# Seven-product matrix multiplication in a token mixer: the third of seven products is itself computed by seven, and the second weights' even and odd rows get separate buffers

## The chip, the cores and the metric

The kernel runs on one core of one Trainium2 chip. The metric is the device time of one execution in microseconds (us). One core has TensorE (matmuls, called PE in the profile; PEld is its weight load), VectorE (DVE), ScalarE (ACT), GpSimd (POOL), SyncE (SP, which here only issues transfers) and DMA engines. All timed executions quoted here are with a granted TensorE clock of 0.999 or 1.0.

## The reference, cut to what matters

Two blocks run one after the other: linear attention, then a token mixer. Only the second half of the mixer (the code calls it mixer 2) is touched:

```python
u = einsum("bsd,sf->bdf", layernorm(h), w1) + b1      # mixer 1
u = gelu(u)
y = einsum("bdf,fs->bds", u, w2) + b2                 # mixer 2: F = 3584, S = 2048, D = 1024
h2 = h + y.transpose(0, 2, 1)
```

## The kernel before

Mixer 2 multiplies w2 by u with a seven-product scheme in the manner of Strassen: a 2x2 block product is done with seven block products in place of eight, at the price of sums of blocks. A `Product7` works on one pair of output row tiles. Its products are p1 to p7: each is 14 matmuls of 128x128 weights by 512 columns. PSUM is the memory in which TensorE accumulates; its matmuls hold one operand (the weights) and stream the other (the moving operand). Products accumulate in place in PSUM tiles A, B, C, so that copying A to B and B to C carries shared partial sums on. The sums of weight blocks (`asums(m)`, for product m) and of the moving operand are made by DVE. A read-out is the operation of DVE or ScalarE that takes the finished partial sum of an inner product out of PSUM; "read-out 7" is that of inner product 7. An evacuation takes a finished output block out and adds the bias.

A product can be computed by seven products again. `Inner` does that for the same product of two neighbouring tile pairs together (a "Quad"): 2 x 14 = 28 wide matmuls become 7 x 7 = 49 matmuls of 256 columns, which is 49 x 256 = 12,544 columns in place of 28 x 512 = 14,336. Products 1 and 5 of mixer 2 are done so in the kernel before. In mixer 2 `Inner.banks` is 2: the inner partial sums a and e are halves of one PSUM tile, b and c halves of another.

```python
class Inner:
    ...
    def i1(self):
        ae = psz.tile([P, BANK], F32, tag="z0", bufs=1, name="psI0")
        bc = psz.tile([P, BANK], F32, tag="z1", bufs=1, name="psI1")
        e = ... if self.banks == 4 else ae
        self.a, self.e, self.b, self.c = ae[:, 0:HW], e[:, HW:CW], bc[:, 0:HW], bc[:, HW:CW]
        self.mm(1, self.a, True)
        act.copy(self.b, self.a)
    def i2(self):
        self.mm(2, self.a, False)
        self.sink(0, 0, self.a)               # read-out 2
    def i5(self): self.mm(5, self.e, True); ...
    def i7(self): self.mm(7, self.c, False); ...   # read-out 7
    def i3(self): self.mm(3, self.b, False); ...
class Inner2(Inner): ...                      # read-outs add into a given tile
```

The narrow matmuls of an inner block are interleaved with wide matmuls of another product ("fill"), in this order:

```python
for f in (n.i1, "b", 0, n.i6, "c", n.i2, 1, n.i5, n.i7, "7", 2, n.i3, "third", 3, n.i4, "end"):
    ...   # an integer is a stretch of fill (9, 7, 5, 7 matmuls here); a name is a place for other engines' work
```

A round of mixer 2 (one Quad; there are three, after a first pair of tile pairs that uses plain products) was:

```python
def run2(self, pend, nxt, on_p4, on_p7, cut):
    ...
    self.interleave(self.in1, self.steps(*[st.p4 for st in pend]))   # inner block of product 1
    on_p4()
    ...
    self.asums(7)
    self.interleave(in5, self.steps(*[st.p6 for st in sts]))         # inner block of product 5
    self.asums(3)
    nxt = nxt()
    for st in sts: st.p2()
    ...
    if nxt is not None: nxt.begin2()      # weight sums of product 5, inner sums of product 1
    for st in sts: st.p7(...)
    on_p7()                               # moving operand of product 4, 2 DVE operations of 2 us
    for st in sts: st.p3()
```

## Time and profile before

| | before |
|---|---|
| time, median (range) | 566.55 us (566.08 to 566.8) |
| TensorE busy | 557.5 of 564.1 us |
| DVE busy | 431.5 us |
| one round of mixer 2 | 40.92 us |

The page of the kernel before: busy time by engine, and the shares of the chain that ended last.

```profile
PE 557.5 (99%) x3215; PEld 303.6 (54%) x3215; DVE 431.5 (76%) x822; ACT 281.5 (50%) x597; POOL 1.8 (0%) x8
...
PE 96%; DVE 2%; ACT 1%; issue 0%; DVEq 0%; ACTq 0%
```

TensorE is in 96% of the chain. This is the chain in order of time around the first round (start in us, duration in us, engine, tile, line, matmuls):

```profile
431.96 0.77 PE psI L217 x7
...
454.75 6.04 PE psA L217 x28
460.79 6.04 PE psC L217 x28
466.83 6.04 PE psB L217 x28
472.88 0.77 PE psI L217 x7
```

These pieces follow one another without a gap, so in mixer 2 the time is simply the sum of the matmuls. It also gives the cadence: 28 wide matmuls take 6.04 us, 216 ns each, and 7 narrow ones 0.77 us, 109 ns each. The Trainium skill, "TensorE: Matmul & The Clock Gate", section "Wait — 56ns, not 53.3ns?", gives N / 2.4 GHz plus about 2.5 ns for a warm matmul, from which 215.8 and 109.2 ns follow as estimates for 512 and 256 columns; the trace agrees with its 216 and 109. The "mean ns" of 379 and 273 that the groups show are lengths of overlapping, pipelined matmuls and no cadence.

What TensorE waited for at inner products in the whole kernel (total us, times, longest):

```profile
PE psI L217 <- DVE t L217: 0.6, 1, 0.6
PE psI L217 <- ACT psI L217: 0.4, 1, 0.4
```

Both are in mixer 1; mixer 2 has none. DVE has room in the first round (its operations in order of time, with the idle time before each in brackets):

```profile
452.85 2.21 DVE L217 TENSOR_TENSOR sa<-wq,sa 128x1792 f16<-128x1792 bf16 x2
458.53 0.43 DVE L217 TENSOR_TENSOR ot<-ot,hr 128x512 bf16<-128x512 bf16 x1 [3.47 <-ACT ot L474]
```

Between 455.1 and 458.5 us DVE had nothing to do. In the second round's first inner block the read-out of inner product 7 also found DVE idle, for 1.24 us:

```profile
480.26 0.43 DVE L217 TENSOR_TENSOR psA<-psI,es 128x256 f32<-128x256 f32 x1 [1.24 <-PE psI L217]
```

### The profile page before, as it was taken

To read this page: it belongs to the slowest core of one execution; us is meant where nothing else is said; L and a number is where in the kernel's file an instruction comes from. 1 tells how busy PE (TensorE), PEld (TensorE's weight loads), DVE (VectorE), ACT (ScalarE), POOL (GpSimd) and SP (SyncE) were. 2 spreads that over 40 slices of the span, in tenths; PEclk is the share of its full clock that TensorE was granted. 3 is DMA by queue.
4 is the path that set the end of the run, shared out by engine and by line. 5 is a ranking of instruction groups with operands and counts; after the bars stand their busy time and mean duration, and the time that the engine had idled before them with its cause. 6 is when DMAs were issued, how large, how long until landed. Compare 5 with 4: busy or idle time off the path is not lost.

```text
span 564.1 us, 8558 instructions
## 1 busy us (share of the span) xinstructions
PE 557.5 (99%) x3215; PEld 303.6 (54%) x3215; DVE 431.5 (76%) x822; ACT 281.5 (50%) x597; POOL 1.8 (0%) x8
## 2 busy tenths in 40 slices
PE   8999999999999999999999999999999999999997
PEld 3444444454444444456667766666445655645643
DVE  6898888544776788888989789888979749658725
ACT  5747777757766877635546465565211311311211
POOL 1000000000000000000000000000000000000000
PEclk9999999999999999999999999999999999999999
DMA  9933332125674852104040340432983922912111
GB/s 304 294 76 75 87 82 38 19 58 194 206 215 123 266 173 80 69 1 125 27 149 21 130 150 1 150 82 50 249 218 94 265 72 75 296 42 74 38 48 46
DMA packets 86089, 67.15 MB, mean 119 GB/s; under 512 B 15762, under 2 KB 80032, under 8 KB 86048
## 3 DMA queue, kind: packets, MB, share of 16 engines
q1 hardware_dynamic: 85312, 65.94, 40.8%
q10 hardware_dynamic: 672, 0.66, 0.3%
q8 instruction: 25, 0.41, 0.3%
q14 instruction: 16, 0.13, 0.1%
q0 software_dynamic: 64, 0.01, 0.0%
HBM read 54.54 MB, written 8.91 MB: 112 GB/s over the span
## 4 chain that ended last, share of the span: by engine, by line
PE 96%; DVE 2%; ACT 1%; issue 0%; DVEq 0%; ACTq 0%
PE psI L217 19%; PE acc_t L217 18%; PE psC L217 15%; PE psB L217 11%; PE psA L217 4%; PE psB L877 4%; PE psC L877 4%; PE psA L877 4%; PE acc_t L801 3%; PE psB L333 2%; PE psA L333 2%; PE acc_t L1152 2%; PE psE L877 2%; PE psC L333 2%; PE kvps L830 1%; PE psE L333 1%
## 5 line engine op out<-in xcount | busy, mean ns | idle before, releaser
L217 PEld LDWEIGHTS <-wq 128*128 128x128 bf16 (+1 forms) x629 | 61.1, 98 | 45.7
L217 PEld LDWEIGHTS <-sa 128*128 128x128 f16 x627 | 61.3, 98 | 36.7 <-issue 0.9
L217 PEld LDWEIGHTS <-is 128*128 128x128 f16 x568 | 55.4, 98 | 27.1 <-issue 1.8
L217 PE MATMUL acc_t<-wo_sb,pqT 128*128 128x512 f16 x256 | 55.6, 379 | 0.0
L217 PE MATMUL psC<-gs,wq 128*128 128x512 f16 (+2 forms) x210 | 44.9, 365 | 0.0
L217 PE MATMUL acc_t<-xnT,wq_sb 128*128 128x512 bf16 x192 | 43.4, 379 | 0.0
L217 PEld LDWEIGHTS <-pqT 128*128 128x128 bf16 x256 | 24.9, 98 | 30.5 <-issue 0.6
L179 DVE TENSOR_SCALAR e_sb<-e_sb 128x512 bf16<-128x512 bf16 x64 | 18.6, 290 | 28.7 <-ACT e_sb L175 28.2
L175 ACT ACTIVATE e_sb<-acc_t 128x512 bf16<-128x512 f32 x40 | 23.9, 597 | 24.5 <-PE acc_t L217 12.0
L217 DVE TENSOR_TENSOR ot<-ot,hr 128x512 bf16<-128x512 bf16 (+2 forms) x27 | 11.2, 414 | 28.1 <-ACT ot L474 27.7
L877 PEld LDWEIGHTS <-xs 128*128 128x128 f16 x208 | 20.0, 98 | 23.4 <-DVE xs L863 1.3
L217 PE MATMUL psC<-hT,sa 128*128 128x512 f16 x112 | 31.2, 379 | 0.0
L217 PEld LDWEIGHTS <-wq_sb 128*128 128x128 bf16 x192 | 18.5, 98 | 23.0 <-issue 1.3
L217 PE MATMUL psI<-hi,is 128*128 128x256 f16 x200 | 30.0, 272 | 0.4 <-ACT psI L217 0.4
L217 PE MATMUL psB<-hT,sa 128*128 128x512 f16 x112 | 29.7, 379 | 0.0
L217 DVE BATCH_NORM_STATS2 hst<-acc_t 128x6 f32<-128x512 f32 x32 | 21.4, 693 | 9.0 <-ACT h_bf L217 8.9
L877 PE MATMUL psA<-wkv,xnT 128*128 128x512 bf16 x104 | 26.7, 379 | 0.0
L877 PEld LDWEIGHTS <-xnT 128*128 128x128 bf16 x156 | 15.3, 98 | 18.5 <-issue 0.2
L217 PE MATMUL psC<-hT,wq 128*128 128x512 f16 x96 | 24.6, 379 | 0.0
L217 ACT CAST h_bf<-acc_t 128x512 bf16<-128x512 f32 x32 | 18.4, 581 | 12.0 <-PE acc_t L217 12.0
L217 ACT COPY psI<-psI 128x256 f32<-128x256 f32 x50 | 18.0, 359 | 11.6 <-PE psI L217 10.5
L176 ACT ACTIVATE r_sb<-acc_t 128x512 bf16<-128x512 f32 x40 | 23.7, 592 | 0.0
(214 smaller groups left out, 1033.5 us busy)
## 6 DMA issues: line engine op xcount, KB each, us to landing
wq<-in_B_w_dram SPq DMA_DIRECT2D x14, 1024.0 KB, 7.9
wq<-in_B_w_dram SPq DMA_DIRECT2D x8, 1792.0 KB, 10.3
xr<-in_A_x_dram SPq DMA_DIRECT2D x16, 256.0 KB, 5.2
rdb<-rd_dram SPq DMA_DIRECT2D x32, 128.0 KB, 4.0
h_dram<-h_bf SPq DMA_DIRECT2D x16, 256.0 KB, 2.0
hr<-h_dram SPq DMA_DIRECT2D x32, 128.0 KB, 2.6
out_dram<-ot SPq DMA_DIRECT2D x31, 128.0 KB, 1.7
x_sb<-in_A_x_dram SPq DMA_DIRECT2D x15, 256.0 KB, 3.1
```

The lines of the kernel that those rows point to most:

```text
L175: pin(nc.scalar.activation(e_sb[:], src, ACT.Exp))
L176: pin(nc.scalar.activation(r_sb[:], src, ACT.Relu))
L179: pin(nc.vector.tensor_scalar(e_sb[:], e_sb[:], 1.0, PHI_EPS, ALU.min, ALU.add))
L217: return (lambda *a, **kw: pin(op(*a, **kw))) if self.always or getattr(Held, self.key) else op
L333: pe.matmul(ps[:, cols], lhsT=lhs[:, k, :], rhs=mv(k)[:, cols], start=(start and k == 0), stop=(k == self.nk - 1), skip_group_check=True,)
L801: mm = nc.tensor.matmul(pp[:, 0:CW], lhsT=xnT[:, kt, i * P:(i + 1) * P], rhs=wkv[:, kt, c * CW:(c + 1) * CW], start=(kt == 0), stop=(kt == ...
L830: pin(nc.tensor.matmul(kv_ps[b][:, sl, :], lhsT=pks[i % NPK][:, j * P:(j + 1) * P], rhs=vaugs[i % NVA][:, j, :], start=False, stop=(i == N ...
L877: pin(nc.tensor.matmul(ps[:], lhsT=lhs[:, k, :], rhs=rhs[:, k, :], start=(start and k == 0), stop=(k == hk2 - 1), skip_group_check=True,))
L1152: nc.tensor.matmul(qp[:, 0:SW], lhsT=wq_sb[:, kt, j * P:(j + 1) * P], rhs=xnT[:, kt, u * SW:(u + 1) * SW], start=(kt == 0), stop=(kt == ND ...
```

## The change

Product 3 is computed by a third inner block (`in3`), interleaved with p2 as fill; p7 moves in front of it. This needs four new sums of the moving operand, once (`sums3`), and four inner sums of weights in each round. Its read-outs are added into the tile e by DVE. The weights of the even row blocks of w2 are free once p7 is through; so they get single buffers that are reloaded there, which makes room for the new tiles. The interleaving order gets one more place for other engines' work, "2", right after inner product 2. The core of the diff, cuts marked, comments added:

```diff
+    def load_w2(p, second):
         nc.sync.dma_start(
-            w2_tiles[p],
-            B_w2[:, p * 2 * P:(p + 1) * 2 * P].rearrange("(k p) s -> p k s", p=P),
+            (odd[p] if second else even[p % 2]),
+            B_w2[:, p * 2 * P:(p + 1) * 2 * P].rearrange("(k two p) s -> p k two s", two=2, p=P)[:, :, second, :],
         )
 ... (cut)
+        def run2(self, pend, on_p4, on_p7, cut, third_sums):
+            def starting():
+                self.asums(5)
+                self.in5 = self.inner(5)
+                self.in5.sums()
+                self.asums(6)
+                for st in sts:
+                    st.begin()
+            self.interleave(self.in1, self.steps(*[st.p4 for st in pend]), {"b": starting}, ...)
             on_p4()
 ... (cut)
             self.asums(7)
-            self.interleave(in5, self.steps(*[st.p6 for st in sts]))
+            self.interleave(self.in5, self.steps(*[st.p6 for st in sts]))
+            third_sums()                       # first round only: four DVE operations
             self.asums(3)
+            in3 = Inner2(sts, 3, self.mov3, "i", self.add_to(e), None)
+            in3.sums()
             for st in sts:
-                st.p2()
+                st.p7()
+                dve.tensor_tensor(st.e[:], st.B[:], st.e[:], ALU.add)
 ... (cut)
+            nxt, halves = on_p7()              # issues the loads of the next even weights
+            halves[0]()                        # product 4's moving operand, first half
+            self.interleave(in3, self.steps(*[st.p2 for st in sts]), {
+                "2": halves[1], "7": begin_next, "third": before_last, "end": ...,
+            }, (("7", None),))
-            for st in sts:
-                st.p3()
```

In the first pair of tile pairs the products stay as they were, but both p7 now come before the last p2, and the next pair's even weights are loaded after them.

More of the change, by code (lines that the diff above doesn't have):

```diff
@@ L152, in load_w1, with w2_view, first_w2 @@
         ))
-    def load_w2(p, pool):
-        w2_tiles[p] = w_tile(pool, WLEN if pool is wpool else NF * 2 * P)[:, 0:NF * 2 * P].rearrange("p (k f) -> p k f", f=2 * P)
+    WH = NFP * 2 * P
+    even, odd = {}, {}
+    def w2_view(t):
+        return t.rearrange("p (k f) -> p k f", f=2 * P)
+    def load_w2(p, second):
         nc.sync.dma_start(
-            w2_tiles[p],
-            B_w2[:, p * 2 * P:(p + 1) * 2 * P].rearrange("(k p) s -> p k s", p=P),
-        )
+            (odd[p] if second else even[p % 2]),
+            B_w2[:, p * 2 * P:(p + 1) * 2 * P].rearrange("(k two p) s -> p k two s", two=2, p=P)[:, :, second, :],
+        )
+    def first_w2(p):
+        t = w_tile(wpool, WLEN)
+        even[p], odd[p] = w2_view(t[:, 0:WH]), w2_view(t[:, WH:2 * WH])
+        odd[p + 4] = odd[p]
+        for second in (0, 1):
+            load_w2(p, second)
     def combine(e, o, t2, t3, t4, v=nc.vector):
@@ L303, with __init__ @@
     class Product7:
-        def __init__(self, p, wt, nk, mov):
+        def __init__(self, p, w, nk, mov):
             self.p, self.nk, self.mov = p, nk, mov
-            v = wt.rearrange("p (k two) (h f) -> p k two h f", two=2, h=2)
-            self.a11 = v[:, :, 0, 0, :]
-            self.a12 = v[:, :, 1, 0, :]
-            self.a21 = v[:, :, 0, 1, :]
-            self.a22 = v[:, :, 1, 1, :]
+            (self.a11, self.a21), (self.a12, self.a22) = [[v[:, :, h * P:(h + 1) * P] for h in range(2)] for v in w]
             self.lhs = {1: self.a11, 2: self.a12, 4: self.a22}
@@ L352, in p1 @@
             act.copy(self.B[:], self.A[:])
-        def shared_tile(self):
-            self.e = cpool.tile([P, BANK], F32, tag=f"e{self.p % 2}", name="e1")
         def p5(self, ks=None):
@@ L361, in p5 @@
             if self.whole(ks):
-                self.shared_tile()
                 act.copy(self.e[:], self.E[:])
@@ L378, in after, with p2 @@
                 late.append(f)
-        def p2(self, ks=None):
+        def p2(self, ks=None, late=None):
             self.mm(2, self.A, False, ks)
             if self.whole(ks):
-                self.evac(0, 0, self.A)
+                self.after(partial(self.evac, 0, 0, self.A), late)
         def p7_fill(self, ks=None, late=None):
@@ L389, in p7_fill, with p7, split @@
                 late.append(partial(self.evac_shared, 1, self.C))
-        def p7(self, cut=None):
+        def p7(self):
             self.mm(7, self.C, False)
             self.parts = [(0, CW, self.C)]
-            if cut is not None:
-                self.parts = [(0, cut, self.C), (cut, CW, psw.tile([P, BANK], F32, tag="w", name="psC2"))]
-                act.copy(self.parts[1][2][:, cut:CW], self.C[:, cut:CW])
             self.evac_shared(1, self.C)
+        def split(self, cut):
+            self.parts = [(0, cut, self.C), (cut, CW, psx.tile([P, BANK], F32, tag="x", name="psC2"))]
+            act.copy(self.parts[1][2][:, cut:CW], self.C[:, cut:CW])
         def p3(self):
@@ L419, in __init__ @@
             c = (p % 2) * 2 * P
-            super().__init__(p, w1_tiles[p // 2][:, :, c:c + 2 * P], NSP, hmov)
+            w = w1_tiles[p // 2][:, :, c:c + 2 * P].rearrange("p (k two) f -> p k two f", two=2)
+            super().__init__(p, (w[:, :, 0, :], w[:, :, 1, :]), NSP, hmov)
         def evac(self, fh, dh, ps, a=0, b=CW):
@@ L450, in __init__ @@
         def __init__(self, p):
-            super().__init__(p, w2_tiles[p], NFP, gmov)
+            super().__init__(p, (even[p % 2], odd[p]), NFP, gmov)
             self.hr = {}
@@ L485, in nop, with share @@
         pass
+    def share(sts):
+        t = cpool.tile([P, 2, BANK], F32, tag="e", name="e1")
+        for s, st in enumerate(sts):
+            st.e = t[:, s, :]
+        return t[:]
     class Quad:
@@ L532, in interleave @@
             for f in (
-                n.i1, "b", 0, n.i6, "c", n.i2, 1, n.i5, n.i7, "7", 2, n.i3, "third", 3, n.i4, "end",
+                n.i1, "b", 0, n.i6, "c", n.i2, "2", 1, n.i5, n.i7, "7", 2, n.i3, "third", 3, n.i4, "end",
             ):
@@ L563, in inner @@
             }[m]
-            n = Inner(self.sts, m, mov, "i", sink, sink_sum)
-            n.sums()
-            return n
-        def begin2(self):
-            self.asums(5)
-            self.in1 = self.inner(1)
-        def run2(self, pend, nxt, on_p4, on_p7, cut):
-            sts = self.sts
-            for st in sts:
-                st.begin()
-            in5 = self.inner(5)
-            self.asums(6)
-            self.interleave(self.in1, self.steps(*[st.p4 for st in pend]))
-            on_p4()
+            return Inner(self.sts, m, mov, "i", sink, sink_sum)
@@ new lines, in run2 @@
+        def run2(self, pend, on_p4, on_p7, cut, third_sums):
+            sts = self.sts
+            def starting():
[5 more added lines that the diff above has]
+                    st.begin()
+            self.interleave(
+                self.in1, self.steps(*[st.p4 for st in pend]), {"b": starting}, (("b", None), ("7", None), ("end", None))
+            )
+            on_p4()
+            e = share(sts)
+            for st in sts:
+                st.fetch(1, 1)
@@ L580, in run2 @@
             for st in sts:
-                st.shared_tile()
                 st.fetch(0, 0)
-            for sh, dh in ((1, 1), (0, 1)):
-                for st in sts:
-                    st.fetch(sh, dh)
+                st.fetch(0, 1)
             self.asums(7)
-            self.interleave(in5, self.steps(*[st.p6 for st in sts]))
+            self.interleave(self.in5, self.steps(*[st.p6 for st in sts]))
+            third_sums()
             self.asums(3)
-            nxt = nxt()
+            in3 = Inner2(sts, 3, self.mov3, "i", self.add_to(e), None)
@@ L590, in run2 @@
+            in3.sums()
             for st in sts:
-                st.p2()
+                st.p7()
+                dve.tensor_tensor(st.e[:], st.B[:], st.e[:], ALU.add)
+            if cut is not None:
+                sts[-1].split(cut)
             for st in sts:
                 st.fetch(1, 0)
-            if nxt is not None:
-                nxt.begin2()
-            for st in sts:
-                st.p7(cut if st is sts[-1] else None)
-            on_p7()
-            for st in sts:
-                st.p3()
+            nxt, halves = on_p7()
@@ new lines, in before_last, with begin_next @@
+            def before_last():
+                if nxt is not None:
+                    nxt.in1.sums(slice(2, 4))
+                sts[0].evac(0, 1, sts[0].e)
+            def begin_next():
+                if nxt is not None:
+                    nxt.in1 = nxt.inner(1)
+                    nxt.in1.sums(slice(0, 2))
+            halves[0]()
+            self.interleave(in3, self.steps(*[st.p2 for st in sts]), {
+                "2": halves[1], "7": begin_next, "third": before_last,
+                "end": lambda: self.late.append(lambda: sts[1].evac(0, 1, sts[1].e)),
+            }, (("7", None),))
@@ L606, in run_first @@
                 st.p1()
+            share(sts)
             for st in sts:
                 st.p2()
-                st.shared_tile()
             before_inner(slice(0, 2))
@@ L673, in run1 @@
             nxt = nxt()
-            for st in sts:
-                st.shared_tile()
+            share(sts)
             if third_sums is not None:
@@ L1477, in load @@
             else:
-                load_w2(0, wpool)
+                first_w2(0)
         return load
@@ L1499 @@
     pools["sa"] = ctx.enter_context(tc.tile_pool(name="sapool2", bufs=4, side="right", reuse_waits="tile"))
-    w2b = ctx.enter_context(tc.tile_pool(name="w2b", bufs=2, side="right", reuse_waits="tile"))
+    w2b = ctx.enter_context(tc.tile_pool(name="w2b", bufs=1, side="right", reuse_waits="tile"))
     g2pool = ctx.enter_context(tc.tile_pool(name="g2pool", bufs=1, side="right", reuse_waits="tile"))
@@ L1503 @@
     inner2 = ctx.enter_context(tc.tile_pool(name="inner2", bufs=1, side="right", reuse_waits="tile"))
-    pools["i"], pools["is_bufs"] = inner2, 7
+    pools["i"], pools["is_bufs"] = inner2, 8
     H2 = NFP // 2
@@ L1516, in derived, with make @@
     def derived(m, of, mend=None):
-        def make():
-            ts = [g2pool.tile([P, H2, CW], FP16, tag=f"gs{h}", name=f"gs{h}") for h in range(2)]
-            for h, sl in enumerate(spans):
-                dve.tensor_tensor(ts[h][:], *of(sl), ALU.subtract)
-                if mend is not None:
-                    mend(ts[h], sl)
-            gmov[m] = lambda k: ts[k // H2][:, k % H2, :]
-        return make
+        ts = []
+        def make(h):
+            if h == 0:
+                ts[:] = [g2pool.tile([P, H2, CW], FP16, tag=f"gs{i}", name=f"gs{i}") for i in range(2)]
+                now = ts[:]
+                gmov[m] = lambda k: now[k // H2][:, k % H2, :]
+            dve.tensor_tensor(ts[h][:], *of(spans[h]), ALU.subtract)
+            if mend is not None:
+                mend(ts[h], spans[h])
+        return [partial(make, h) for h in range(2)]
     def less_b11(t, sl):
@@ L1533, with run_all, next2, after_p7 @@
     make_t4 = derived(4, lambda sl: (gO[:, sl, 0:CW], gT2[:, sl, :]))
-    load_w2(1, wpool)
+    first_w2(1)
     for p in (2, 3):
-        load_w2(p, w2b)
+        odd[p] = odd[p + 4] = w2b.tile([P, NFP, 2 * P], BF16, tag=f"o{p}", name=f"w2o{p}")[:]
+        load_w2(p, 1)
     mov1, sums1 = inner_moving(gE[:, :, 0:CW], NFP, inner2, "gi1")
     mov5, sums5 = inner_moving(gE[:, :, CW:D], NFP, inner2, "gi5")
+    mov3, sums3 = inner_moving(gO[:, :, CW:D], NFP, inner2, "gi3")
     def quad2(u):
-        return Quad([Mixer2(2 * u), Mixer2(2 * u + 1)], mov1, mov5)
+        return Quad([Mixer2(2 * u), Mixer2(2 * u + 1)], mov1, mov5, None, mov3)
+    def run_all(fs):
+        for f in fs:
+            f()
     def after_p4(u):
         def act():
-            make_t3()
+            run_all(make_t3)
             for p in (2 * u + 2, 2 * u + 3):
                 if 4 <= p < NSP:
-                    load_w2(p, wpool if p % 4 < 2 else w2b)
+                    load_w2(p, 1)
         return act
+    def next2(u):
+        for p in (2 * u, 2 * u + 1):
+            load_w2(p, 0)
+        return quad2(u)
+    def after_p7(u):
+        return lambda: (next2(u + 1) if 2 * u + 2 < NSP else None, make_t4)
     pend = [cur, Mixer2(1)]
-    nxt = quad2(1)
+    share(pend)
     for st in pend:
@@ L1560 @@
                 st.asum(m)
-            make_t3_raw()
+            run_all(make_t3_raw)
         st.p1()
         st.p5()
-        st.p2()
+        if st is not pend[1]:
+            st.p2()
         st.p6()
-        if st is pend[1]:
-            st.asum(3)
+    pend[1].asum(3)
     sums1()
@@ L1570 @@
     for st in pend:
+        st.p7()
+    for st in pend:
         st.fetch(1, 0)
-    nxt.begin2()
-    for st in pend:
-        st.p7()
-    make_t4()
+    nxt = next2(1)
+    run_all(make_t4)
+    pend[1].p2()
+    nxt.in1 = nxt.inner(1)
+    nxt.in1.sums()
     for st in pend:
@@ L1580 @@
         cur = nxt
-        last = 2 * u + 2 == NSP
         pend, nxt = cur.run2(
-            pend, lambda: None if last else quad2(u + 1), after_p4(u), make_t4, CW - P if last else None,
+            pend, after_p4(u), after_p7(u), CW - P if 2 * u + 2 == NSP else None, sums3 if u == 1 else nop,
         )
+    while Quad.late:
+        Quad.late.pop(0)()
     for st in pend:
```

## The prediction

> **What bounds it.** TensorE. In the chain of waits every piece from 392 to 560.8 us is a matmul, without a gap; the table of stretches has it busy for all of 400 to 550 us at granted clock 1.00. From the chain: 28 matmuls of 512 columns take 6.04 us (216 ns each), 7 of 256 take 0.765 us (109 ns). A round of mixer 2 (two output tiles) takes 40.92 us (431.96, 472.88, 513.79, 554.71).
>
> **Removed, added.** In each of three rounds the third product (28 wide matmuls, 6.04 us) becomes seven inner products (49 narrow, 5.36 us): 0.685 us a round, 2.05 us in all. The first pair keeps its work, only its order changes; the tail is unchanged.
>
> The price is DVE work. Per round: four inner sums (0.62 us each), four accumulations (three at 0.43, one about 0.75), two additions of the shared term (0.75 each), less two 0.75 us evacuations: about +5.2 us on 28 busy in 41. Once: 4.3 us of moving sums. DVE has room on average; the question is where it queues.
>
> **Critical path.** Two inner products share a PSUM bank. The Trainium skill, "PSUM — Partial Sum Buffer", section "PSUM bank collisions raise a hardware error", says to guard PSUM by bank, not by address. The changed kernel's instruction listing agrees: inner product 5 waits for the read-out of 2, and 3 for that of 7. Read-out 2 was ScalarE's; in the new block it is DVE's, in fixed order behind other work. I added up DVE work with durations and spacings of the old trace (estimates):
>
> - First round: from 452.85 us DVE has moving sums 4.3, product sums 2.0, inner sums 2.3, read-outs of product 7 with the shared additions 3.6, half of the next moving operand 1.95, and only then read-out 2, at about 467.0 us. TensorE wants inner product 5 at 466.55: with the read-out's 0.43, about 1.0 us of stall. The operand's second half delays read-outs 5 and 7: about 0.35 us more before inner 3.
> - Rounds 2 and 3: two late additions and product 5's weight sums (2.1 us) now fall inside the first inner block. Read-out 7 ends about 8.6 us into it, inner 3 is wanted at 8.36: about 0.3 us each. The new block itself fits there (slack 0.6 us).
>
> Sum: 2.05 saved, 1.9 given back. Even weights, single buffered: 0.9 MB each, issued as each product 7 ends. 1.8 MB took about 10 us here; I estimate 5 to 6 us to landing, wanted about 9 us after product 7. No stall.
>
> **Prediction.** My sum says almost nothing; its errors are several tenths of a us, and an order placed this carefully probably misses some of these stalls. I settle on 566.0 us, 8 in 10 between 564.7 and 566.9. Faster by over 2%: 0.005; within 2%: 0.99; slower: 0.005.
>
> **What would show it.** The chain stays nearly all TensorE, with 63 matmuls more. A round without stalls would last 40.24 us; I expect the first near 41.5, the others near 40.6. In the waits: TensorE on DVE, about 1 us before inner 5 and 0.3 us before inner 3 of the new block in the first round, about 0.3 us before inner 3 of the first block in rounds 2 and 3. No TensorE wait for the even weights. DVE busy +19 to 20 us.
>
> **What would make it wrong.** DVE reaching read-out 2 in time in the first round: then about 564.7. Even weights landing later than 9 us after product 7: DVE would stand in front of read-out 3, costing 1 to 3 us a round. Narrow matmuls of the new block pacing slower than 109 ns.

## The result, and the profile after

| | before | changed |
|---|---|---|
| time, median (range), 4 runs each | 566.55 us (566.08 to 566.8) | 567.42 us (566.92 to 567.89) |
| ratio of the fast runs | | 1.0016 (95%: 0.9999 to 1.0034) |
| TensorE busy / matmuls | 557.5 us / 3215 | 556.7 us / 3278 |
| DVE busy | 431.5 us | 448.5 us |
| rounds 1, 2, 3 of mixer 2 | 40.92, 40.91, 40.91 us | 42.85, 40.50, 40.48 us |

Ratios here are the mean time of one kernel's fast runs over that of the other's of the same rounds, so not quite the ratio of the medians. A round is counted in the trace from the start of its first narrow matmul to that of the next round; the last one to the start of the last fourth product. "Mixer 2" below runs from its first matmul to the end of its last: 165.25 us before, 166.33 after. The profiled execution of the changed kernel is 2.0 us longer in span than that of the kernel before, but 0.9 us of this lies in front of mixer 2: in its chain a load of attention weights at 15 us stands, and every later piece of the attention block comes 0.9 us later. A repeat of the changed kernel (below) does not have it. So mixer 2 is compared by its own length. The interval of the ratio includes 1: by the times alone the changed kernel is not shown to be slower than the kernel before.

The page of the changed kernel:

```profile
PE 556.7 (98%) x3278; PEld 309.8 (55%) x3278; DVE 448.5 (79%) x853; ACT 287.6 (51%) x609; POOL 1.8 (0%) x8
...
PE 84%; DVE 10%; DMA 3%; issue 1%; ACT 1%; SPq 0%; DVEq 0%; ACTq 0%
```

DVE now has 10% of the chain, where it had 2%. This is the length of the path that leads through DVE and not lost time: TensorE's delays in mixer 2, worked out below, are 3.2 us in all. What TensorE waited for at the new or moved places:

```profile
PE psI L229 <- DVE e L229: 1.2, 2, 0.9
...
PE psI L229 <- DVE psA L229: 0.9, 1, 0.9
```

The first line is the new block (two waits), the second the first block. **First inner block of round 1** (timeline: start, duration, engine, line, operation, output<-inputs; SPq is a transfer's issue, `x5` five operations merged):

```profile
423.82 0.38 SPq L161 DMA_DIRECT2D wq<-in_B_w_dram  x1
...
430.73 0.62 DVE L254 TENSOR_TENSOR is<-wq 128x896 f16<-128x896 bf16 x1 [2.73 <-DMA wq<-in_B_w_dram]
...
439.63 2.08 DVE L229 TENSOR_TENSOR sa<-sa,wq 128x1792 f16<-128x1792 f16 x2
...
439.97 1.24 PE L229 MATMUL psC<-gs,wq 128*128 128x512 f16 x5
...
441.64 0.42 DVE L229 TENSOR_TENSOR psA<-psI,es 128x256 f32<-128x256 f32 x1
...
442.11 0.92 PE L229 MATMUL psI<-gE,is 128*128 128x256 f16 x7 [0.90 <-DVE psA L229]
```

The even weights' second load is issued at 423.82 us, as the second p7 ends, and DVE, which has waited 2.73 us for it, goes on at 430.73, 6.9 us after the issue. Everything behind it is late, so the 2.08 us of weight sums for product 6 (439.63) stand just in front of the read-out of inner product 7 (441.64). The five wide matmuls at 439.97 take 5 x 0.216 = 1.08 us; inner product 3 was due at 441.05 and started at 442.11, at the moment that the read-out let it: 1.06 us late.

**New inner block of round 1**, from the end of the block of product 5 on:

```profile
454.81 1.08 DVE L229 TENSOR_TENSOR gi<-gO 128x1792 f16<-128x1792 f16 x1
...
458.18 1.09 DVE L229 TENSOR_TENSOR gi<-gO,gi 128x1792 f16<-128x1792 f16 x1
459.19 2.09 DVE L229 TENSOR_TENSOR sa<-w2o,sa 128x1792 f16<-128x1792 bf16 x2
...
466.82 1.67 PE L229 MATMUL psA<-gO,w2o 128*128 128x512 f16 x7
...
467.02 2.01 DVE L229 TENSOR_TENSOR gs<-gO,gT 128x3584 f16<-128x3584 f16 x1
...
468.95 0.41 DVE L229 TENSOR_TENSOR e<-psI,e 128x256 f32<-128x256 f32 x1
469.29 2.01 DVE L229 TENSOR_TENSOR gs<-gO,gT 128x3584 f16<-128x3584 f16 x1
469.42 0.92 PE L229 MATMUL psI<-gO,is 128*128 128x256 f16 x7 [0.93 <-DVE e L229]
...
470.94 1.24 PE L229 MATMUL psA<-gO,w2o 128*128 128x512 f16 x5
471.22 1.24 DVE L229 TENSOR_TENSOR e<-psI,e 128x512 f32<-128x512 f32 x2
...
472.51 0.93 PE L229 MATMUL psI<-gO,is 128*128 128x256 f16 x7 [0.32 <-DVE e L229]
```

The four moving sums (454.81 to 459.27) fill the hole that DVE had in the kernel before. Work after them is late by as much; at 467.02 the first half of product 4's operand starts, and only at 468.95 read-out 2. The seven wide matmuls that started at 466.82 end their cadence at 468.33, when inner product 5 was due; it started at 469.42, 1.09 us late. The second half of the operand (469.29) then delays read-outs 5 and 7 (471.22), and inner product 3 starts at 472.51 instead of 470.94 + 1.08 = 472.02: another 0.49 us.

That inner product 5 waits for read-out 2, which reads the other half of the same PSUM tile, goes with the shared tile. In mixer 1 `Inner.banks` is 4, so that the inner sums have separate tiles, and DVE does the read-outs of two of its inner blocks in the same way. In the same execution, in the block of its product 3:

```profile
276.48 0.60 PE L229 MATMUL psI<-hO,is 128*128 128x256 f16 x4
...
277.62 1.87 DVE L229 TENSOR_TENSOR t<-psI,t 128x256 f32<-128x256 f32 x4
```

Inner product 5 started at 276.48, 1.14 us before DVE began the first of the four read-outs merged here, number 2 (277.62). No run gave mixer 2 separate tiles.

**Rounds 2 and 3** lose only at inner product 3 of the first block; in round 2:

```profile
481.69 2.08 DVE L229 TENSOR_TENSOR sa<-sa,wq 128x1792 f16<-128x1792 f16 x2
...
482.82 1.24 PE L229 MATMUL psC<-gs,w2o 128*128 128x512 f16 x5
...
483.70 0.42 DVE L229 TENSOR_TENSOR psA<-psI,es 128x256 f32<-128x256 f32 x1
...
484.17 0.92 PE L229 MATMUL psI<-gE,is 128*128 128x256 f16 x7
```

Again the weight sums for product 6 (481.69) stand in front of read-out 7 (483.70). Due at 482.82 + 1.08 = 483.90, inner product 3 started at 484.17: 0.27 us. Round 3 has the same 0.27. The list of waits above does not show these two at all.

Round 1 loses 1.06 + 1.09 + 0.49 = 2.64 us and lasts 42.85, against 40.22 for the matmuls alone (what experiment 4 measures without any stall). Three rounds save 2.08 us against the kernel before and give back 2.64 + 0.27 + 0.27 = 3.18: 1.1 us lost, which is the difference of the two lengths of mixer 2.

### The profile page after: what moved, and what is told of

Read it like the earlier page. It is cut to its first block, busy times and chain, and to the rows that moved or that the text cites. A ratio compares the mean times of both kernels' runs of the same rounds, so it can differ in the third digit from the quotient of the medians.

```text
span 566.1 us, 8738 instructions
## 1 busy us (share of the span) xinstructions
PE 556.7 (98%) x3278; PEld 309.8 (55%) x3278; DVE 448.5 (79%) x853; ACT 287.6 (51%) x609; POOL 1.8 (0%) x8
## 4 chain that ended last, share of the span: by engine, by line
PE 84%; DVE 10%; DMA 3%; issue 1%; ACT 1%; SPq 0%; DVEq 0%; ACTq 0%
PE psI L229 19%; PE acc_t L229 18%; PE psC L229 11%; PE psB L229 8%; PE psB L904 4%; PE psC L904 4%; PE psA L904 4%; PE psA L229 4%; DVE sa L229 2%; PE acc_t L1179 2%; PE psE L904 2%; DVE is L229 2%; PE psC L341 2%; PE psA L341 2%; PE acc_t L828 2%; DMA wkv<-in_A_wqkv_dram 1%
## 5 line engine op out<-in xcount | busy, mean ns | idle before, releaser
L229 PEld LDWEIGHTS <-is 128*128 128x128 f16 x652 | 63.6, 98 | 33.2 <-issue 5.6
L229 PEld LDWEIGHTS <-sa 128*128 128x128 f16 x606 | 59.3, 98 | 28.8 <-issue 0.9
L229 PEld LDWEIGHTS <-wq 128*128 128x128 bf16 (+1 forms) x503 | 49.2, 98 | 32.6
L229 PE MATMUL psC<-gs,wq 128*128 128x512 f16 x140 | 32.0, 379 | 0.0
L229 ACT COPY psI<-psI 128x256 f32<-128x256 f32 x50 | 17.9, 359 | 11.7 <-PE psI L229 10.6
L828 PE MATMUL acc_t<-wkv,xnT 128*128 128x512 bf16 x96 | 21.6, 379 | 0.9 <-ACT xnT L1081 0.9
```

The source lines that it names most:

```text
L229: return (lambda *a, **kw: pin(op(*a, **kw))) if self.always or getattr(Held, self.key) else op
L828: mm = nc.tensor.matmul(pp[:, 0:CW], lhsT=xnT[:, kt, i * P:(i + 1) * P], rhs=wkv[:, kt, c * CW:(c + 1) * CW], start=(kt == 0), stop=(kt == ...
```

## The experiments

The theory (A): the loss is DVE's order. Read-outs that TensorE waits for stand in a fixed queue behind work that is wanted later; in round 1 this is made worse by even weights that land late. Rivals: (B) DVE simply has too much work, so that the order can only move the wait; (C) the single-buffered even weights hold TensorE in every round. The first four runs shared one chip and nine runs of the kernel before (median 566.5 us), the last four another (566.34 us).

### 1. The changed kernel again

No edit.

> The changed kernel once more, as the measure for the three runs beside it. All theories: about 567.4 us, 0.9 above the kernel before; on TensorE mixer 2 lasts about 166.2 us from its first matmul to its last (before: 165.1), the first round 42.9 us, rounds 2 and 3 40.5 us each.

Measured: 566.77 us, ratio 1.001 (0.9997 to 1.0022). Rounds 42.52, 40.50, 40.48 us; mixer 2 took 166.01 us. The two stalls of the new block and the 0.27 of rounds 2 and 3 repeat to within 0.01 us. Only the stall at the first block of round 1 differs: 0.74 in place of 1.06 us. There the weights came 6.6 us after their issue, 0.3 us sooner than in the other profile.

### 2. Weight sums of product 6 behind the read-outs

```diff
                 self.in5.sums()
-                self.asums(6)
 ...
-                self.in1, self.steps(*[st.p4 for st in pend]), {"b": starting}, ...
+                self.in1, self.steps(*[st.p4 for st in pend]),
+                {"b": starting, "third": lambda: self.asums(6)}, ...
```

> Only an order changes: the sums of the weights for product 6 (two DVE operations, 2.1 us) go from in front of the read-outs of inner products 7 and 3 of a round's first inner block to behind them. Theory A (DVE order: read-outs that TensorE waits for stand behind work that is wanted later): the stalls before inner product 3 of the first block go, 1.06 us in round 1 and 0.26 in rounds 2 and 3, so rounds of about 41.8, 40.25, 40.25 us, mixer 2 about 164.6, the kernel about 565.8 us. Rival B (DVE has too much work in all; the order only moves the wait): the same work remains, so within 0.3 us of the changed kernel. Rival C (the single-buffered even weights land late and hold TensorE in every round): rounds 2 and 3 unchanged at 40.5.

Measured: 565.55 us, ratio 0.9987 (0.9974 to 0.9999). Rounds 41.80, 40.22, 40.21 us. DVE's operations in the first block of round 1:

```profile
439.98 0.43 DVE L229 TENSOR_TENSOR psA<-psI,es 128x256 f32<-128x256 f32 x1 [0.95 <-PE psI L229]
...
442.09 2.08 DVE L229 TENSOR_TENSOR sa<-sa,wq 128x1792 f16<-128x1792 f16 x2
```

Read-out 7 (439.98) now finds DVE idle, although the even weights came late here too: 6.5 us after their issue (6.9 and 6.6 us in the two executions above), and DVE waited 2.3 us for them. The sums follow at 442.09. All three stalls of the first blocks are gone, the two of the new block remain (1.09 and 0.49). So for rounds 2 and 3 the whole loss was the order of these operations, and C falls for these rounds.

### 3. Half of the moving sums earlier

```diff
-            self.interleave(self.in5, self.steps(*[st.p6 for st in sts]))
-            third_sums()
+            self.interleave(self.in5, self.steps(*[st.p6 for st in sts]), {"7": lambda: third_sums(slice(1, 2))})
+            third_sums(slice(2, 4))
 ...
     pend[1].p2()
+    sums3(slice(0, 1))
     nxt.in1 = nxt.inner(1)
```

> Only an order changes: of the four moving sums of the new inner block (1.09 us each) one goes to the first pair of tiles, where DVE waits for weights anyway, one into DVE's gap between the read-outs of inner products 7 and 3 of the second inner block; two stay. Theory A: read-out 2 of the new block comes in time in round 1, its two stalls (1.09 and 0.48 us) go, round 1 about 41.3 us, rounds 2 and 3 unchanged at 40.5, the kernel about 565.8 us. Rival B: no gain beyond 0.3 us. Rival C: no change.

Measured: 565.4 us, ratio 0.9984 (0.9972 to 0.9997). Rounds 40.77, 40.49, 40.49 us. The two stalls of the new block are gone; in the first blocks 0.55 (round 1), 0.28 and 0.28 us remain. Round 1 is better than expected because its other stall was smaller in this execution, in which the weights came 6.1 us after their issue. Whether the edit, which puts one sum in front of that wait, has a part in this was not tested.

### 4. Both reorderings

The edits of 2 and 3 together.

> Both reorderings together, the same work. Theory A: no TensorE stall is left in mixer 2, three rounds of about 40.25 us, mixer 2 about 163.1 us, the kernel about 564.4 us, which beats the kernel before by about 2.1. Rival B: stalls come back elsewhere, the sum of the rounds stays above 122.7 us (the kernel before). Rival C: about 0.26 us a round remains in rounds 2 and 3.

Measured: 564.45 us, ratio to the kernel before 0.9962 (0.9948 to 0.9976). Rounds 40.22, 40.22, 40.21 us; mixer 2 took 163.16 us. DVE around read-out 2 of the new block in round 1:

```profile
466.07 0.42 DVE L229 TENSOR_TENSOR e<-psI,e 128x256 f32<-128x256 f32 x1 [0.24 <-PE psI L229]
466.41 2.02 DVE L229 TENSOR_TENSOR gs<-gO,gT 128x3584 f16<-128x3584 f16 x1
```

Read-out 2 (466.07) now waits 0.24 us for TensorE, not TensorE for it. What TensorE waits for at inner products is back to mixer 1's two lines:

```profile
PE psI L229 <- DVE t L229: 0.6, 1, 0.6
PE psI L229 <- ACT psI L229: 0.3, 1, 0.3
```

DVE is busy for 448.1 us, as in the changed kernel (448.5), and every stall is gone. B falls: the work fits, the order did not.

### 5. Both second products of the first pair behind its products 7

```diff
         st.p5()
-        if st is not pend[1]:
-            st.p2()
         st.p6()
 ...
-    pend[1].p2()
+    for st in pend:
+        st.p2()
```

> Only TensorE's order in the first pair of tiles changes: both second products go behind both products 7, so that the even weights of the next pair are free, and loaded, about 3 us earlier. Theory A with its second part (in round 1 the even weights land too late for DVE, which then reaches the read-out late): DVE's wait of 2.7 us for the weights goes, and with it the stall before inner product 3 of round 1's first block (0.74 to 1.07 us); round 1 about 41.85 us (its two stalls in the new block, 1.58 us, stay), rounds 2 and 3 40.5; the kernel about 0.8 us under the changed one. If the landing has no part: no change.

Measured: 566.18 us, ratio 0.9996 (0.9983 to 1.0008). Rounds 41.79, 40.50, 40.49 us: the first block's stall in round 1 is gone, the others stay. One part of the expectation missed: DVE still waits 2.03 us for the weights.

```profile
420.45 0.34 SPq L477 DMA_DIRECT2D out_dram<-ot  x1
...
421.31 0.45 SPq L161 DMA_DIRECT2D wq<-in_B_w_dram  x1
...
427.65 0.63 DVE L254 TENSOR_TENSOR is<-wq 128x896 f16<-128x896 bf16 x1 [2.03 <-DMA wq<-in_B_w_dram]
...
439.75 0.43 DVE L229 TENSOR_TENSOR psA<-psI,es 128x256 f32<-128x256 f32 x1
```

The second load was issued at 421.31, behind an output store in the same queue that waits for DVE (420.45), and DVE itself now arrives earlier. But DVE goes on at 427.65 and not at 430.73, and read-out 7 comes at 439.75. What counts is when the weights land, not whether DVE waits for them. So in round 1 the landing is a cause, and the order of the sums for product 6 another: taking away either (run 2 or this one) removes the stall. This run changes TensorE's order too; four traces without such a change, compared in "Why the prediction was wrong", show the same for the landing.

### 6. The third product wide again, all else as changed

```diff
-            in3 = Inner2(sts, 3, self.mov3, "i", self.add_to(e), None)
-            in3.sums()
 ... (cut: p7, fetch, halves as before, without the additions into e; tile psC2 of the last product moves to another PSUM pool)
+            for st in sts:
+                st.p2()
+            if nxt is not None:
+                nxt.in1 = nxt.inner(1)
+                nxt.in1.sums()
+            for st in sts:
+                st.p3()
```

> The new order and the split weight buffers stay, the third product is one wide product again (same result). Theory A: the 1.58 us of stalls in the new block and the 0.27 of rounds 2 and 3 go with it, the late even weights of round 1 stay (0.7 to 1.1 us): round 1 about 41.8 us, rounds 2 and 3 at 40.92 as in the kernel before; mixer 2 about 166.1 us, the kernel about 0.9 us above the kernel before. Rival C (split single buffers cost something in every round): rounds 2 and 3 over 41.2 us.

Measured: 567.12 us, ratio 1.0011 (0.9999 to 1.0024). Rounds 41.59, 40.91, 40.91 us; mixer 2 took 165.92 us. The one stall left is 0.68 us before inner product 3 of the first block in round 1. So the split buffers and the new order cost 0.67 us in mixer 2, all of it by the late weights of round 1, and nothing in rounds 2 and 3: C holds for round 1 alone. The third product itself saved about 2.08 us and cost 1.58 in the new block and 0.54 in the first blocks of rounds 2 and 3: about zero.

### 7. The moving operand of product 4 later

```diff
-            halves[0]()
 ...
                     nxt.in1.sums(slice(2, 4))
+                halves[1]()
                 sts[0].evac(0, 1, sts[0].e)
 ...
-                "2": halves[1], "7": begin_next, "third": before_last,
+                "2": halves[0], "7": begin_next, "third": before_last,
```

> Another cure for the first round's new block: the two halves of product 4's moving operand (2.0 us of DVE each) go behind the read-outs they stood in front of, the first behind read-out 2, the second behind read-out 3. Theory A: the two stalls of the new block go (1.58 us), but the second half now stands in front of product 5's weight sums of the next round, so the stall before inner product 3 of the first block in rounds 2 and 3 grows from 0.27 to about 1.3 us: rounds of about 41.2, 41.5, 41.5 us, the kernel within 0.6 us of the changed one, rather slower. If DVE had room at that place: rounds 2 and 3 stay at 40.5 and the kernel gains 1.5 us.

Measured: 569.41 us, ratio 1.0052 (1.0038 to 1.0065). Rounds 40.83, 42.29, 42.30 us. The stalls of the new block are gone, as expected, and the one of rounds 2 and 3 grew, but to 2.08 us and not to 1.3. So the kernel came 2.0 us above the changed one's median (2.6 above that of its repeat), where at most 0.6 was expected. In round 2:

```profile
472.19 2.02 DVE L229 TENSOR_TENSOR gs<-gO,gT 128x3584 f16<-128x3584 f16 x1
...
475.99 0.42 DVE L229 TENSOR_TENSOR ot<-ot,hr 128x512 bf16<-128x512 bf16 x1 [0.78 <-ACT ot L480]
...
480.05 1.24 PE L229 MATMUL psC<-gs,w2o 128*128 128x512 f16 x5
...
483.21 0.93 PE L229 MATMUL psI<-gE,is 128*128 128x256 f16 x7 [1.92 <-DVE psA L229]
```

The operand's second half (472.19) also pushed back read-out 4, and with it ScalarE's last evacuation, for which DVE then stood idle (0.78 us before 475.99) with the weight sums behind it. The cure moved the wait and enlarged it. A gap in DVE's time is worth using only if what stands behind it is not wanted at once.

### 8. Runs 4 and 5 together

> Both reorderings of DVE and the new TensorE order of the first pair. If no stall is left in mixer 2 with the two reorderings alone, the third adds nothing: mixer 2 163.1 to 163.2 us, the kernel about 564.4 us, within 0.3 us of the run with the two.

Measured: 563.99 us, ratio to the kernel before 0.9957 (0.9945 to 0.997). Rounds 40.22, 40.22, 40.22 us; mixer 2 took 163.16 us, the same as in run 4. As expected the third reordering adds nothing to mixer 2; here DVE does not wait for the weights of the next pair at all. The page:

```profile
PE 555.3 (99%) x3278; PEld 309.9 (55%) x3278; DVE 448.0 (80%) x853; ACT 287.7 (51%) x609; POOL 1.8 (0%) x8
...
PE 96%; DVE 2%; ACT 1%; issue 0%; DVEq 0%; ACTq 0%
```

TensorE has 96% of the chain again. Runs 4 and 8 compute the reference's result and beat both kernels, by 2.1 and 2.4 us against the medians of the kernel before: 0.4%, with intervals clear of 1.

## Why the prediction was wrong

The measured median of 567.42 us lies above the stated range of 564.7 to 566.9, and above the point of 566.0. The comparison within 2% was right. For the kernel a gain of about 0.55 us was settled on; mixer 2 alone, where the change saves and costs, became 1.09 us longer (0.76 in the repeat). Step by step:

- **TensorE bounds mixer 2; 0.685 us a round are to be had.** Right. Without stalls a round took 40.22 us (predicted 40.24) against 40.92. The narrow matmuls kept their 109 ns. That the chain "stays nearly all TensorE" did not hold: 84% (86% in the repeat).
- **Where DVE would queue.** Right, and nearly right in size. New block of round 1: "a stall of about 1.0" and "about 0.35 us more"; measured 1.09 and 0.49. Rounds 2 and 3: "about 0.3 us each"; measured 0.27. Their length was predicted at 40.6 and measured at 40.50 and 40.48. The first round was predicted near 41.5 and lasted 42.85; without the stall of the next point it would have been 41.79, which is what run 5 measured.
- **"Even weights ... No stall."** This step failed, in both of its terms. The landing was taken as 5 to 6 us; DVE could go on 6.9 us after the issue (6.6 in the repeat). The lead, "wanted about 9 us after product 7", holds for the later rounds only: in the first pair DVE reached the sums that need the weights at 428.0 us, 4.2 us after the second p7. DVE waited 2.7 us there, and inner product 3 of the first block came 1.06 us late (0.74 in the repeat). Four traces with the same order up to this place (changed, repeat, runs 6 and 7) show how the two go together: DVE went on 6.91, 6.58, 6.51 and 6.44 us after the second issue, and the stall was 1.06, 0.74, 0.68 and 0.61 us; the difference is 5.83 to 5.85 us each time. So, as an estimate from these traces, the stall is what the landing takes beyond about 5.84 us: the predicted 5 to 6 us would have cost at most about 0.2 us even with the short lead. Why the landing took longer was not traced. The prediction had named late weights as a danger, but in front of read-out 3 of the new block, and in every round; experiment 6 shows it in round 1 alone.
- **"An order placed this carefully probably misses some of these stalls".** This failed too. The sum had come out at 2.05 saved and 1.9 given back, which is about 566.4; the prediction then took about 0.4 us off on trust. But every stall that the sum had named did occur (2.12 us in all). With its own sum and the missing 0.7 to 1.1 us it would have stood at 567.1 to 567.5.
- **DVE busy +19 to 20 us.** 17.0 us. Most of the difference is a slip: the items that the prediction lists for a round (2.48 for inner sums, 2.04 for accumulations, 1.5 for additions, less 1.5) make 4.5 us and not its 5.2, so 17.9 us in all. It also counted four accumulations a round where the trace has five, which goes the other way. Printed durations overlap by up to 0.1 us from one operation to the next, but that is the smaller part: added up one by one over the trace they rose by 17.5 us. The rest was not traced.
- **How much of the miss is chance.** The result lies 0.5 us above the range, and the repeat, with 566.77, inside it. The two profiled executions (567.89 and 566.77) differ by 1.12 us: 0.78 lies in front of mixer 2, and 0.33 is the smaller stall in round 1. The other executions have no trace. Executions of one kernel lie up to 1.4 us apart here (run 6), so the time alone would not have shown which step was wrong; the stalls in the traces do.

## What to carry to other kernels

When a change takes matmuls away and gives DVE more to do, free DVE time on average says little: list DVE's operations in order between two read-outs that TensorE waits for, and put sums that are wanted later behind them. Work that is done once (here four moving sums in the first round, and a first load with less lead than all later ones) needs its own sum, since the steady round does not show it. Moving work off one wait can lengthen another, as in run 7: ask what stands behind the new place in the same queue.

## What the Trainium skill lacked or had wrong

- "PSUM — Partial Sum Buffer", section "PSUM bank collisions raise a hardware error", says to guard PSUM by bank. It puts no number on what this costs where two accumulators share a bank and a matmul waits for a read-out of the other half. Here this coupled TensorE to DVE's queue, with waits of 0.27 to 2.08 us at single places. Mixer 1, with separate tiles of a bank's size, did not wait: its inner product 5 started 1.14 us before read-out 2. No run gave mixer 2 separate banks.
- No page of the skill says by how much an "idle before" of TensorE in such a profile falls short of the delay. The ends of matmuls are modelled in it: the waits printed as 0.93 and 0.32 us were delays of 1.09 and 0.49 us by the starts of the matmuls and their cadence, and delays of 0.27 us were not printed as waits.
- "VectorE: DVE Perf Modes", section "The DRAIN you can't avoid", says that a next operation does not start until the pipe is empty, and that one that is not held starts earlier. The trace puts a number on it: an independent operation starts before the printed end of the one in front (2.01 us printed, 1.93 us from start to start), a dependent one just after it (0.62 printed, 0.65 to 0.66). So a sum of printed durations can come out higher than the time taken.
